# Block-sparse attention with a gated MLP: key and query loads ahead of values, a fourth raw buffer in the weight tile, one more probability buffer, split sums of squares

## Chip, core and metric

The kernel runs on one core of a Trainium2 chip. The metric is the device time of one execution in microseconds; lower is better. TensorE (PE) does matmuls and transposes, VectorE (DVE), ScalarE (ACT) and GpSimd (POOL) do the rest, and SyncE (SP) issues most of the DMAs. Each engine works through its own instructions in the order in which the program emits them.

## The reference

The inputs are q, k and v with batch 4, 8 heads, 768 positions and head size 64, a table of 3 sampled key blocks for each of 24 query blocks, and three weight matrices. All inputs but the table are 32-bit floats.

```python
scores = scale * np.matmul(q, k.transpose(0, 1, 3, 2))
# mask: window of one block, first and last block rows and columns, sampled blocks
scores = np.where(mask, scores, -1000000000.0)
attn = softmax(scores)
x = (attn @ v) as [B * S, H * D]           # 3072 x 512
xn = x / np.sqrt(np.mean(x * x, -1) + 1e-06) * rms_g
g = xn @ w_gate                            # 512 x 1536
out = (g * sigmoid(g) * (xn @ w_val)) @ w_out
```

## The kernel before, in words

Positions are laid out as 128 partitions by 6 columns. Heads are taken in pairs: each batch has 4 pairs, so g = 0 to 15 counts all pairs. The mask is not added to the scores: 24 extra rows of the contraction carry it, so keys and queries of a pair are cast into a tile `aug` of 88 used rows and then transposed into `X`. For batch 0 (pairs 0 to 3) PE transposes (`tpx`, L257) and a copy from PSUM follows (`evx`); the second half of the columns of the batch's queries comes by one load, `q2` (L227), and is cast and transposed later. For pairs 4 to 15 one DMA transpose a pair does it (`turn`, L243). Values are cast into `vaug` with a column of ones (`pad_v`).

The work is cut into 10 units: unit u has a batch and 1 or 3 query tiles of 128 (units 0 to 2 one each, unit 3 the other three tiles of batch 0, then two units of three tiles for each later batch). For every unit and pair there are score groups (`qk`, L275, two PSUM banks), exponentials on ACT (`exp`, L290), the product with the values (`av`, L304) and the division (`xo`, L315 and L316, DVE). Then come the sum of squares (`sq`, L326, DVE), its power -0.5 (`rsq`, L333, POOL), the scaled rows (`xq`, L340, DVE) and their transposition: for units 0 to 3 on PE with a copy (`tr`, L351, and `cp`, L359), for units 4 to 9 by a DMA transpose on SP's queue (`xt`, L366). The constant NPET is the first unit of the second kind. The MLP follows in groups f: `g` and `v` (L378), `th` (tanh, L387, ACT), `uu` (L393) and `hp` (L404, DVE), then `y` (L417) and the output (`yo`).

The order on each engine is made by a planner at build time. Every step is entered by `op` with the engines that may do it and a time for each, its dependences, a priority, and the buffers it takes and gives back; the planner picks the step that could start first, with priority breaking near ties. For DMAs a fixed list `seq` gives the order on SP's queue, in which DMA transposes stand where the planner puts them. What is planned is emitted in that order; the times in the plan are only for choosing.

Three buffers of the pool `raw` hold keys, queries and values as loaded. Pairs 0 to 2 of batch 0 have one each. Pair 3 takes the buffer of pair 0 (`load3`), so its load waits until pair 0's keys, queries and values have been cast. The weights are loaded by POOL in eight chunks of 384 columns (`wi`, L209) and two of `w_out` (L213). A small copy on POOL (`gate_pool`, L230) holds the first chunk until a load has landed; the third and fourth pair of chunks also wait for `rsq` of units 0 and 1. On SP a tiny DMA (`gate_sync`, L219) that reads a weight holds back the loads of pairs 4 to 7. The 40 unused columns of `aug` are cleared by POOL (`zero_pad`, L249) before pair 4 is cast.

Idle matmuls on a zero tile (L129) stand where the planner expects gaps on PE before 24 us.

Of the kernel before, what the change touches and what calls it, by code (L numbers as in the profile page):

```python
# [9 lines left out]
FP32 = mybir.dt.float32  # L10
BF16 = mybir.dt.bfloat16
# [6 lines left out]
def kernel(  # L18
# [12 lines left out]
    nc = tc.nc  # L31
# [14 lines left out]
    AHEAD, HURRY, HURU = 0.8, ("av", "xo", "sq", "rsq", "xq", "tr", "cp"), 0  # L46
    NSTARV = 3
    AH = {"uu": 0.3, "hp": 0.3}
# [51 lines left out]
    load0(1, 0)  # L100
    load0(0, 2)
    load0(1, 1)
# [126 lines left out]
    def gate_pool(g):  # L229
        nc.gpsimd.tensor_copy(out=scf, in_=A[g][:, 1, 0, 0:1])  # L230

# [14 lines left out]

    def zero_pad():
        for t in aug:
            nc.gpsimd.memset(t[:, :, :, :, KQ:P], 0.0)  # L249

# [29 lines left out]
    def exp(u, pr, g):  # L280
        b, c0, nt = UNITS[u]
        kt, w = KT[nt], nt * P
        if (u, pr) not in pts:
            if nt == 1:
                t_ = work.tile([P, 2, NC, 2, w], BF16, name="pt", tag="pt", bufs=NPT)
# [4 lines left out]
        nc.scalar.activation(  # L290
            out=pts[u, pr][:, g * kt:(g + 1) * kt].rearrange("p j e w -> p e j w"),
            in_=s_[:, :, 0:kt * w].rearrange("p e (j w) -> p e j w", w=w),
            func=AF.Exp, scale=SCALE)
# [26 lines left out]
    def sq(u, t):  # L320
        nt = UNITS[u][2]
        if u not in mss:
            mss[u] = work.tile([P, nt], FP32, name="ms", tag="ms")
        sc = work.tile([P, DM], BF16, name="sc", tag="sc", bufs=1)
        x = xos[u][:, t].rearrange("p h d -> p (h d)")
        nc.vector.tensor_tensor_reduce(  # L326
            out=sc, in0=x, in1=x, scale=1.0 / DM, scalar=1e-6, op0=ALU.mult, op1=ALU.add,
            accum_out=mss[u][:, t:t + 1])

    def rsq(u):  # L330
        nt = UNITS[u][2]
        r = work.tile([P, nt], FP32, name="rs", tag="rs")
        nc.gpsimd.tensor_tensor(out=r, in0=mss[u], in1=nhalf[:, 0:nt], op=ALU.pow)  # L333
        mss[u] = r
# [97 lines left out]

    NPT, NXN, NHP, NPET = 3, 3, 2, 4
    pools = {n: [0.0] * c for n, c in (
# [28 lines left out]

    def load3(e, p):
        A.append(raw.tile([P, 3, 2, NC * D], FP32, name="qkv", tag="qkv"))
        load0(3, 0)

# [3 lines left out]
    ld0(("l", 1, 0), 1.0)  # L471
    ld0(("l", 0, 2), 1.1)
    ld0(("l", 1, 1), 0.6)
    for g, i in ((2, 0), (2, 1), (1, 2), (3, 0), (3, 1), (2, 2), (3, 2)):
        ld0(("l", g, i), 0.6 if i == 1 else 1.1,
            load3 if (g, i) == (3, 0) else lambda e, p, g=g, i=i: load0(g, i),
            [], [("raw", 3)] if (g, i) == (3, 0) else [])
    ld0(("lg",), 0.7, lambda e, p: nc.sync.dma_start(
# [6 lines left out]
    for i in range(NWC + NOC):  # L485
        for m in range(2 if i < NWC else 1):
            def wi(e, p, i=i, m=m):
                if i + m == 0:
                    gate_pool(3)
                load_w(i, m) if i < NWC else load_wo(i - NWC)  # L490
            op(("wi", i, m), {"POOL": 0.9 + 0.2 * (i + m == 0)},
               [prev] if prev else [("l", 3, 0)], (2, i, m), wi)
            if (i, m) in ((2, 0), (3, 0)):
                made["wi", i, m]["deps"] += [("rsq", i - 2)]
            prev = ("wi", i, m)
        if i == 0:
            ld0(("q2",), 2.2, q2_, [], [("hp", ("q2",))])
            op(("w0",), {"DMA": 2.1}, [("wi", 0, 0)], (0,), None)
            seq.append(("w0",))
        op(("w", i), {"DMA": 4.2 if i else 2.1}, [prev], (0,), None)  # L500
        seq.append(("w", i))
        if i >= NWC - 1:
            seq += [("ld", NP + i - NWC + 1, j) for j in range(3)]
# [5 lines left out]
    for g in range(NP):  # L509
        a_ = g % NAUG  # L510
        rr = [("raw", g)]
        if g:
# [9 lines left out]
        for i in range(2):  # L522
            for n_, (es, lo, hi) in enumerate((KP, QP)[i][g == 0]):
                m_ = len(es) * (hi - lo)
                if i == 0:
                    pri = (-1, g, 0.5 + 0.1 * n_ + (g == 0 and lo == 3))
                else:
                    pri = (-1, g, 1) if lo == 0 else (2.5, g, lo)
                res = f"aK{a_}" if i == 0 else f"a{'QR'[lo == 3]}{a_}"
                key = ("tp", g, i, es[0], lo)  # L530
                op(key, {"PE": m_ * 0.056}, [("fq", g, lo)] if i else [("fk", g)] if g else [],
                   pri, lambda e, p, a=(g, i, es, lo, hi): tpx(*a, p),
                   [(TP1[:1] if i and lo == 3 else TP1, key), (f"X{g}", g)],
                   [(res, g)] if i == 0 else [(res, (g, lo == 3))])
# [14 lines left out]
    pools["aK0"] = []  # L549
    op(("zp",), {"POOL": 1.8}, [], (9,), lambda e, p: zero_pad(), at=24.0)  # L550
    for g in range(NP, B * NP):
        b, pr = divmod(g, NP)
        gate = {NP: 2, NP + 1: 3, NP + 2: 4, NP + 3: 5}.get(g)
        for i in range(3):
            def ld(e, p, g=g, i=i, gate=gate):
                if gate is not None and i == 0:
                    gate_sync(gate)
                load(g, i)
            op(("ld", g, i), {"DMA": 1.1}, [("w", gate)] if gate is not None and i == 0 else [],
               (1,), ld, [("raw", g)] if i == 0 else [])  # L560
            if i < 2:
                op(("fill", g, i), {"DVE": 0.57}, [("ld", g, i), ("zp",)] + [
                    ("tp", g_, i_, 0, 3 * i_) for g_ in (2, 3) for i_ in range(2)],
                   (4, g, i), lambda e, p, g=g, i=i: fill(g, i, e), [(f"aug{g % NAUG}", (g, False))])
# [16 lines left out]
    for u, (b, c0, nt) in enumerate(UNITS):  # L581
        w, last = nt * P, c0 + nt == NC
        ng = NC // KT[nt]
        for pr in range(NP):
            g0 = b * NP + pr
            pk = pr // 2 if nt == 1 else pr
            for g in range(ng):
                op(("qk", u, pr, g), {"PE": 2 * KT[nt] * mm(w)}, dep0(g0, b, c0, nt, KT[nt], g),
                   (2 if u else 0.5, u, pr, g), lambda e, p, a=(u, pr, g): qk(*a, p),
                   [(S3 if u < NOPEN else S_, ("s", u, pr, g)), ("pt", (u, pk))],  # L590
                   [(f"X{g0 % NSLOT}", g0)] if last and g == ng - 1 else [])
# [6 lines left out]
               lambda e, p, a=(u, pr): av(*a, p), [([(7,)] + [(6,)] * (u < 3), ("o", u, pr)), ("xo", u)],  # L598
               ([("pt", (u, pk))] if nt > 1 or pr % 2 else []) + ([(f"va{b % 2}", b)] if last and pr == NP - 1 else []))
            op(("xo", u, pr), {"DVE": 0.4 + w / 960.0}, [("av", u, pr)], (0, u, pr),  # L600
               lambda e, p, a=(u, pr): xo(*a), [], [(None, ("o", u, pr))])
        for t in range(nt):
            op(("sq", u, t), {"DVE": 0.75}, [("xo", u, pr) for pr in range(NP)], (1, u, t),
               lambda e, p, a=(u, t): sq(*a))
        op(("rsq", u), {"POOL": 0.9}, [("sq", u, t) for t in range(nt)], (0, u), lambda e, p, u=u: rsq(u))
        for t in range(nt):
# [82 lines left out]
    while ready:  # L689
# [27 lines left out]
        for names, key, nme in got:  # L717
# [11 lines left out]
        end[o["key"]] = fin + (  # L729
            3.7 if o["key"] == ("q2",) else 8.0 if o["key"][0] == "ld" and o["key"][1] >= NP else 4.0 if o["key"][0] == "turn"  # L730
            else LAT[e])
# [54 lines left out]
```

The softmax here doesn't subtract the row's maximum and nothing guards it: scores larger than these inputs give would overflow.

## Time and profile before

| what | value |
|---|---|
| median of 4 runs | 313.0 us (312.28 to 313.95) |
| profiled execution | 313.95 us |
| its span in the trace | 312.2 us |
| mean granted TensorE clock | 0.995 |
| PE waits for DVE, ACT in all | 3.8 us and 0.6 us |
| DMA queue of SP | 64800 packets, 37.23 MB |
| landing of a 384 KB load of keys, of values (median) | 4.6 us, 6.1 us |
| landing of a DMA transpose into `XA`, into `xn` (median) | 7.1 us, 3.7 us |

The span runs from the first to the last instruction of the trace. A group of instructions is given by line, engine, operation and tiles, with its count, busy time and mean. The sliced rows cut the span into 40 equal parts of 7.8 us; each digit is a busy share in tenths. PEclk is the granted clock of PE in tenths of full. The matmul ends are modelled, so busy time of PE is not a measure of how well it is used. In a timeline a line has start, duration, engine, line of code, operation and, in brackets, the idle time before it and what ended it.

### The profile page before, as it was taken

What the parts mean: (1) busy time and instruction counts of PE and PEld (TensorE: products, weight loads), DVE (VectorE), ACT (ScalarE), POOL (GpSimd) and SP (SyncE); (2) the same over time, 40 slices, a digit from 0 to 9 for tenths busy, and PEclk for the clock granted to TensorE, in tenths of its full rate; (3) what the DMA queues carried; (4) which work ended last, traced back from release to release, by engine and by line L of the source; (5) the groups of instructions that cost most, each with busy time, mean ns of one, the idle gap of its engine ahead of it and who ended that gap; (6) DMA issues with size and microseconds to landing.
All of it is one profiled execution on the core that took longest, in us unless ns stands there. A gap on an engine that the chain in (4) does not pass through costs nothing.

```text
span 312.2 us, 7395 instructions
## 1 busy us (share of the span) xinstructions
PE 303.9 (97%) x3063; PEld 201.8 (65%) x3063; DVE 191.1 (61%) x423; ACT 207.1 (66%) x325; POOL 24.6 (8%) x42
## 2 busy tenths in 40 slices
PE   8799999999999999999999999999999999999995
PEld 7798887866666666666666666666666546556543
DVE  5559655786666878766664853674488707727500
ACT  5958987678888777878787687878733233323222
POOL 3355500010000101000000100010001000000000
PEclk9979999999999999999999999999999999999999
DMA  6999999999999799951785030012000041010022
GB/s 206 304 236 166 168 267 236 164 300 294 252 258 240 255 208 251 285 177 36 151 140 100 34 84 4 34 21 66 2 34 3 6 121 60 0 68 2 0 104 101
DMA packets 70661, 42.42 MB, mean 136 GB/s; under 512 B 48356, under 2 KB 67556, under 8 KB 70628
## 3 DMA queue, kind: packets, MB, share of 16 engines
q1 hardware_dynamic: 64800, 37.23, 48.4%
q0 software_dynamic: 5792, 4.72, 10.0%
q8 instruction: 24, 0.39, 0.5%
q14 instruction: 9, 0.07, 0.1%
q10 hardware_dynamic: 36, 0.00, 0.0%
HBM read 28.57 MB, written 6.29 MB: 112 GB/s over the span
## 4 chain that ended last, share of the span: by engine, by line
PE 91%; DMA 3%; ACT 2%; DVE 1%; SPq 1%; issue 1%; ACTq 0%; DVEq 0%
PE PS L378 40%; PE PS L417 20%; PE PS L275 18%; PE PS L304 11%; DMA qkv<-in_k_dram 2%; DMA qkv<-in_v_dram 2%; ACT pt L290 2%; SPq L93 1%; PE PS L257 1%; PE PS L351 0%; ACT th L387 0%; DVE uu L393 0%; DVE aug L113 0%; ACT XA L109 0%; DVE vaug L113 0%
## 5 line engine op out<-in xcount | busy, mean ns | idle before, releaser
L290 ACT ACTIVATE pt<-PS 128x768 bf16<-128x768 f32 x192 | 145.6, 813 | 37.7 <-PE PS L275 36.2
L393 DVE SCALAR_TENSOR_TENSOR uu<-th,PS 128x384 bf16<-128x384 bf16 x96 | 53.2, 554 | 62.1 <-ACT th L387 59.9
L275 PE MATMUL PS<-XA 88*128 88x384 bf16 (+1 forms) x480 | 81.9, 296 | 0.7 <-ACT pt L290 0.6
L378 PE MATMUL PS<-xn,wg 128*128 128x384 bf16 (+1 forms) x480 | 75.4, 294 | 0.4 <-DVE uu L393 0.4
L378 PE MATMUL PS<-xn,wv 128*128 128x384 bf16 (+1 forms) x480 | 75.5, 293 | 0.0
L417 PE MATMUL PS<-wo,hp 128*128 128x512 bf16 (+1 forms) x300 | 70.4, 370 | 0.0
L387 ACT ACTIVATE th<-PS 128x384 bf16<-128x384 f32 x96 | 47.3, 493 | 33.0 <-PE PS L378 30.6
L404 DVE TENSOR_TENSOR hp<-uu,PS 128x384 bf16<-128x384 bf16 x96 | 51.4, 551 | 15.2 <-PE PS L378 14.4
L378 PEld LDWEIGHTS <-wg 128*128 128x128 bf16 x480 | 41.6, 97 | 24.1 <-issue 1.0
L378 PEld LDWEIGHTS <-wv 128*128 128x128 bf16 x480 | 41.5, 97 | 23.3 <-issue 0.2
L275 PEld LDWEIGHTS <-XA 88*128 88x128 bf16 x480 | 40.0, 99 | 21.6 <-issue 1.5
L417 PEld LDWEIGHTS <-hp 128*128 128x128 bf16 x300 | 29.0, 98 | 26.9
L304 PEld LDWEIGHTS <-pt 128*128 128x128 bf16 x1152 | 41.8, 98 | 6.0 <-issue 0.7
L304 PE MATMUL PS<-vaug,pt 128*128 128x65 bf16 x1152 | 43.3, 194 | 0.6 <-DVE xo L316 0.6
L427 ACT ACTIVATE yo<-PS 128x512 f32<-128x512 f32 (+1 forms) x23 | 13.3, 579 | 28.0 <-PE PS L417 27.1
L333 POOL TENSOR_TENSOR rs<-ms,nhalf 128x3 f32<-128x3 f32 (+1 forms) x10 | 7.8, 785 | 201.5 <-DVE ms L326 201.5
L316 DVE TENSOR_TENSOR xo<-PS,rz 128x384 f32<-128x384 f32 (+1 forms) x40 | 19.1, 478 | 1.4
L340 DVE SCALAR_TENSOR_TENSOR xq<-xo,rs,gB 128x512 bf16<-128x512 f32 x24 | 17.5, 754 | 0.2 <-POOL rs L333 0.2
L315 DVE RECIPROCAL rz<-PS 128x6 f32<-128x6 f32 (+1 forms) x40 | 7.4, 185 | 16.1 <-PE PS L304 16.0
L113 DVE CAST aug<-qkv 128x768 bf16<-128x768 f32 (+2 forms) x30 | 15.2, 524 | 3.1 <-DMA qkv<-in_k_dram 2.7
L326 DVE CUSTOM_DVE_ANT_0 sc<-xo 128x512 bf16<-128x512 f32 x24 | 16.5, 687 | 0.3
L257 PE MATMUL PS<-ident,aug 128*88 128x128 bf16 x96 | 8.4, 239 | 1.9 <-DVE XA L113 1.7
(54 smaller groups left out, 70.1 us busy)
## 6 DMA issues: line engine op xcount, KB each, us to landing
qkv<-in_v_dram SPq DMA_DIRECT2D x16, 384.0 KB, 6.1
out_dram<-yo SPq DMA_DIRECT2D x23, 256.0 KB, 2.0
qkv<-in_k_dram SPq DMA_DIRECT2D x15, 384.0 KB, 4.6
qkv<-in_q_dram SPq DMA_DIRECT2D x12, 384.0 KB, 4.7
wg<-in_moe_w_gate_dram POOLq DMA_DIRECT2D x4, 384.0 KB, 6.6
wv<-in_moe_w_val_dram POOLq DMA_DIRECT2D x4, 384.0 KB, 8.1
wo<-in_moe_w_out_dram POOLq DMA_DIRECT2D x2, 768.0 KB, 17.4
q<-in_q_dram SPq DMA_DIRECT2D x1, 768.0 KB
```

The costliest lines, as they stand in the source:

```text
L113: nc.vector.tensor_copy(out=out, in_=in_)
L275: nc.tensor.matmul(out=s_[:, e, j * w:(j + 1) * w], lhsT=x[0:KQ, 0, e, jt * P:(jt + 1) * P], rhs=x[0:KQ, 1, e, c0 * P:c0 * P + w], start=T ...
L290: nc.scalar.activation(out=pts[u, pr][:, g * kt:(g + 1) * kt].rearrange("p j e w -> p e j w"), in_=s_[:, :, 0:kt * w].rearrange("p e (j w) ...
L304: nc.tensor.matmul(out=o_[:, t, e, :], lhsT=pt[:, jt, e, t * P:(t + 1) * P], rhs=va[:, (2 * pr + e) * NC + jt, 0:D + 1], start=(jt == 0), ...
L316: nc.vector.tensor_tensor(out=xos[u][:, :, 2 * pr:2 * pr + 2, :], in0=o_[:, :, :, 0:D], in1=rz.unsqueeze(3).to_broadcast([P, nt, 2, D]), o ...
L326: nc.vector.tensor_tensor_reduce(out=sc, in0=x, in1=x, scale=1.0 / DM, scalar=1e-6, op0=ALU.mult, op1=ALU.add, accum_out=mss[u][:, t:t + 1])
L340: nc.vector.scalar_tensor_tensor(out=xqs[u][:, t, :], in0=xos[u][:, t].rearrange("p h d -> p (h d)"), scalar=mss[u][:, t:t + 1], in1=gB, o ...
L378: nc.tensor.matmul(out=p_[:, j, :].rearrange("p (t w) -> p t w", w=P), lhsT=w_[:, c, f_ * P:(f_ + 1) * P], rhs=xns[u][:, :, c, :], start=( ...
L387: nc.scalar.activation(out=t_, in_=tiles["gp", u, f], func=AF.Tanh, scale=0.5)
L393: nc.vector.scalar_tensor_tensor(out=t_, in0=tiles.pop(("th", u, f)), scalar=1.0, in1=tiles.pop(("gp", u, f)), op0=ALU.add, op1=ALU.mult)
L404: nc.vector.tensor_tensor(out=hps[u][:, f * fg:(f + 1) * fg, :], in0=tiles.pop(("uu", u, f)), in1=tiles.pop(("vp", u, f)), op=ALU.mult)
L417: nc.tensor.matmul(out=tiles["yp", u, t, h], lhsT=hps[u][:, f, t * P:(t + 1) * P], rhs=wo[:, f, x], start=(f == 0), stop=(f == NF - 1))
```

## The change

Loads of batch 0 are issued in the order k0, q0, k1, q1, k2, q2, k3, q3, then v0 to v3; before, v0 stood ahead of q1, and v1 ahead of k3. Pair 3's raw data lie in the first 4608 columns of the tile `wo`, seen as 32-bit floats, which the load of `w_out` fills later; `load3` and its wait for a buffer are gone. The first weight chunk waits for the values of pair 1 instead of the queries of pair 3.

The probabilities of pairs 2 and 3 of unit 0 are put into a buffer of the pool `hp` (`ph`), so units 0 to 2 have four such buffers and not three. For units 0 to 2 the sum of squares is taken in two instructions, the first over the first three pairs, the second over the last pair with the first result as its start. The columns of `aug` are cleared by DVE, one tile at a time, not before 32 us of the plan. The copies of the second half of the queries of pairs 0 to 3 can be done by DVE only, and their transposes may use a second PSUM bank. Gate groups of unit 3 may use a second bank. NPET is 2, so the transposes of units 2 and 3 go by DMA on SP's queue. The plan reckons with 2.6 us from issue to landing for the later loads of batch 0.

In the program that results PE has 16 transposes (L351) and 2 idle matmuls fewer. All casts of the second half of the queries are on POOL. In SP's queue unit 2's DMA transpose stands directly behind the load `q2` and ahead of the gate and loads of pair 4. Behind it come the loads of pairs 4 and 5, `turn` of pairs 4 and 5, an output, and then the gate and three loads of pair 6, the gate and the keys of pair 7, unit 3's DMA transpose, an output, two loads of pair 7, three of pair 8 and `turn` of pair 6. On PE the first matmuls with values come behind 13 of the score groups, where it was 5. The order of the first gate group of unit 3 and the score groups of pairs 5 and 6 has also moved.

```diff
-    load0(0, 2)
     load0(1, 1)
...
-        nc.gpsimd.tensor_copy(out=scf, in_=A[g][:, 1, 0, 0:1])
+        nc.gpsimd.tensor_copy(out=scf, in_=A[g][:, 2, 0, 0:1])
...
-    def zero_pad():
-        for t in aug:
-            nc.gpsimd.memset(t[:, :, :, :, KQ:P], 0.0)
+    def zero_pad(i):
+        nc.vector.memset(aug[i][:, :, :, :, KQ:P], 0.0)
...
+                if u == 0 and pr == 2:
+                    t_ = work.tile([P, NF, 3 * P], BF16, name="ph", tag="hp", bufs=NHP)
...
+        i, z = 0 if nt == 1 else t, slice(0, DM)
+        if nt == 1:
+            z = (slice(0, 3 * DM // 4), slice(3 * DM // 4, DM))[t]
+        x = xos[u][:, i].rearrange("p h d -> p (h d)")[:, z]
         nc.vector.tensor_tensor_reduce(
-            out=sc, in0=x, in1=x, scale=1.0 / DM, scalar=1e-6, op0=ALU.mult, op1=ALU.add,
-            accum_out=mss[u][:, t:t + 1])
+            out=sc[:, z], in0=x, in1=x, scale=1.0 / DM, scalar=mss[u][:, 0:1] if nt == 1 and t else 1e-6,
+            op0=ALU.mult, op1=ALU.add, accum_out=mss[u][:, t:t + 1])
...
-    NPT, NXN, NHP, NPET = 3, 3, 2, 4
+    NPT, NXN, NHP, NPET = 3, 3, 2, 2
...
-    def load3(e, p):
-        A.append(raw.tile([P, 3, 2, NC * D], FP32, name="qkv", tag="qkv"))
-        load0(3, 0)
+    A.append(wo.rearrange("p f x -> p (f x)")[:, 0:12 * NC * D].bitcast(FP32).rearrange(
+        "p (i e x) -> p i e x", i=3, e=2))
...
-    for g, i in ((2, 0), (2, 1), (1, 2), (3, 0), (3, 1), (2, 2), (3, 2)):
+    for g, i in ((2, 0), (2, 1), (3, 0), (3, 1), (0, 2), (1, 2), (2, 2), (3, 2)):
...
-               [prev] if prev else [("l", 3, 0)], (2, i, m), wi)
+               [prev] if prev else [("l", 1, 2)], (2, i, m), wi)
...
-                   [(TP1[:1] if i and lo == 3 else TP1, key), (f"X{g}", g)],
+                   [(TP1[:2] if i and lo == 3 else TP1, key), (f"X{g}", g)],
...
-                elif i and lo == 3 or g == 0 and lo == 0:
+                elif g == 0 and lo == 0:
...
-    op(("zp",), {"POOL": 1.8}, [], (9,), lambda e, p: zero_pad(), at=24.0)
+    for i in range(2):
+        op(("zp", i), {"DVE": 0.4}, [], (9,), lambda e, p, i=i: zero_pad(i), at=ZPAT)
...
-               lambda e, p, a=(u, f): proj(*a, wg, "gp", p), [([(4,)], ("g", u, f)), ("hp", HG[u])])
+               lambda e, p, a=(u, f): proj(*a, wg, "gp", p), [([(4,)] + [(6,)] * (2 < u < NG2), ("g", u, f)), ("hp", HG[u])])
```

More of the change, by code (lines that the diff above doesn't have):

```diff
@@ L46 @@
     AHEAD, HURRY, HURU = 0.8, ("av", "xo", "sq", "rsq", "xq", "tr", "cp"), 0
-    NSTARV = 3
+    NSTARV, ZPAT, NG2 = 3, 32.0, 4
     AH = {"uu": 0.3, "hp": 0.3}
@@ L284, in exp @@
             if nt == 1:
-                t_ = work.tile([P, 2, NC, 2, w], BF16, name="pt", tag="pt", bufs=NPT)
+                if u == 0 and pr == 2:
+                    t_ = work.tile([P, NF, 3 * P], BF16, name="ph", tag="hp", bufs=NHP)
+                    t_ = t_.rearrange("p f w -> p (f w)")[:, 0:4 * NC * w].rearrange(
+                        "p (a j e w) -> p a j e w", a=2, j=NC, e=2)
+                else:
+                    t_ = work.tile([P, 2, NC, 2, w], BF16, name="pt", tag="pt", bufs=NPT)
                 pts[u, pr // 2 * 2], pts[u, pr // 2 * 2 + 1] = t_[:, 0], t_[:, 1]
@@ L322, in sq @@
         if u not in mss:
-            mss[u] = work.tile([P, nt], FP32, name="ms", tag="ms")
+            mss[u] = work.tile([P, max(nt, 2)], FP32, name="ms", tag="ms")
         sc = work.tile([P, DM], BF16, name="sc", tag="sc", bufs=1)
-        x = xos[u][:, t].rearrange("p h d -> p (h d)")
+        i, z = 0 if nt == 1 else t, slice(0, DM)
+        if nt == 1:
+            z = (slice(0, 3 * DM // 4), slice(3 * DM // 4, DM))[t]
+        x = xos[u][:, i].rearrange("p h d -> p (h d)")[:, z]
         nc.vector.tensor_tensor_reduce(
-            out=sc, in0=x, in1=x, scale=1.0 / DM, scalar=1e-6, op0=ALU.mult, op1=ALU.add,
-            accum_out=mss[u][:, t:t + 1])
+            out=sc[:, z], in0=x, in1=x, scale=1.0 / DM, scalar=mss[u][:, 0:1] if nt == 1 and t else 1e-6,
+            op0=ALU.mult, op1=ALU.add, accum_out=mss[u][:, t:t + 1])
     def rsq(u):
@@ L332, in rsq @@
         r = work.tile([P, nt], FP32, name="rs", tag="rs")
-        nc.gpsimd.tensor_tensor(out=r, in0=mss[u], in1=nhalf[:, 0:nt], op=ALU.pow)
+        x = mss[u][:, 1:2] if nt == 1 else mss[u]
+        nc.gpsimd.tensor_tensor(out=r, in0=x, in1=nhalf[:, 0:nt], op=ALU.pow)
         mss[u] = r
@@ L471 @@
     ld0(("l", 1, 0), 1.0)
-    ld0(("l", 0, 2), 1.1)
     ld0(("l", 1, 1), 0.6)
-    for g, i in ((2, 0), (2, 1), (1, 2), (3, 0), (3, 1), (2, 2), (3, 2)):
+    for g, i in ((2, 0), (2, 1), (3, 0), (3, 1), (0, 2), (1, 2), (2, 2), (3, 2)):
         ld0(("l", g, i), 0.6 if i == 1 else 1.1,
-            load3 if (g, i) == (3, 0) else lambda e, p, g=g, i=i: load0(g, i),
-            [], [("raw", 3)] if (g, i) == (3, 0) else [])
+            lambda e, p, g=g, i=i: load0(g, i))
     ld0(("lg",), 0.7, lambda e, p: nc.sync.dma_start(
@@ L488, in wi @@
                 if i + m == 0:
-                    gate_pool(3)
+                    gate_pool(1)
                 load_w(i, m) if i < NWC else load_wo(i - NWC)
             op(("wi", i, m), {"POOL": 0.9 + 0.2 * (i + m == 0)},
-               [prev] if prev else [("l", 3, 0)], (2, i, m), wi)
+               [prev] if prev else [("l", 1, 2)], (2, i, m), wi)
             if (i, m) in ((2, 0), (3, 0)):
@@ L510 @@
         a_ = g % NAUG
-        rr = [("raw", g)]
+        rr = [("raw", g)] if g < NP - 1 else []
         if g:
@@ L561 @@
             if i < 2:
-                op(("fill", g, i), {"DVE": 0.57}, [("ld", g, i), ("zp",)] + [
+                op(("fill", g, i), {"DVE": 0.57}, [("ld", g, i), ("zp", 0), ("zp", 1)] + [
                     ("tp", g_, i_, 0, 3 * i_) for g_ in (2, 3) for i_ in range(2)],
@@ L586 @@
             pk = pr // 2 if nt == 1 else pr
+            ptn = ("hp", "ph") if u == 0 and pk == 1 else ("pt", (u, pk))
             for g in range(ng):
@@ L589 @@
                    (2 if u else 0.5, u, pr, g), lambda e, p, a=(u, pr, g): qk(*a, p),
-                   [(S3 if u < NOPEN else S_, ("s", u, pr, g)), ("pt", (u, pk))],
+                   [(S3 if u < NOPEN else S_, ("s", u, pr, g)), ptn],
                    [(f"X{g0 % NSLOT}", g0)] if last and g == ng - 1 else [])
@@ L598 @@
                lambda e, p, a=(u, pr): av(*a, p), [([(7,)] + [(6,)] * (u < 3), ("o", u, pr)), ("xo", u)],
-               ([("pt", (u, pk))] if nt > 1 or pr % 2 else []) + ([(f"va{b % 2}", b)] if last and pr == NP - 1 else []))
+               ([ptn] if nt > 1 or pr % 2 else []) + ([(f"va{b % 2}", b)] if last and pr == NP - 1 else []))
             op(("xo", u, pr), {"DVE": 0.4 + w / 960.0}, [("av", u, pr)], (0, u, pr),
                lambda e, p, a=(u, pr): xo(*a), [], [(None, ("o", u, pr))])
-        for t in range(nt):
-            op(("sq", u, t), {"DVE": 0.75}, [("xo", u, pr) for pr in range(NP)], (1, u, t),
+        ns = max(nt, 2)
+        for t in range(ns):
+            dq = [("sq", u, 0)] if nt == 1 and t else []
+            d_ = 0.75 if nt > 1 else (0.6, 0.25)[t]
+            op(("sq", u, t), {"DVE": d_}, dq + [("xo", u, pr) for pr in range(NP - (nt == 1 and t == 0))], (1, u, t),
                lambda e, p, a=(u, t): sq(*a))
-        op(("rsq", u), {"POOL": 0.9}, [("sq", u, t) for t in range(nt)], (0, u), lambda e, p, u=u: rsq(u))
+        op(("rsq", u), {"POOL": 0.9}, [("sq", u, t) for t in range(ns)], (0, u), lambda e, p, u=u: rsq(u))
         for t in range(nt):
@@ L729 @@
         end[o["key"]] = fin + (
-            3.7 if o["key"] == ("q2",) else 8.0 if o["key"][0] == "ld" and o["key"][1] >= NP else 4.0 if o["key"][0] == "turn"
+            3.7 if o["key"] == ("q2",) else 2.6 if o["key"][0] == "l" and (o["key"][1] > 1 or o["key"][2] == 2) else 8.0 if o["key"][0] == "ld" and o["key"][1] >= NP else 4.0 if o["key"][0] == "turn"
             else LAT[e])
```

## The prediction

> **What bounds the kernel now.** I read the busy rows and the sliced rows of the page first, then the waits of TensorE, then the first 40 us in the timeline and in windows of 1 us, then the landing times of the DMAs.
>
> ```profile
> PE 303.9 (97%) x3063; PEld 201.8 (65%) x3063; DVE 191.1 (61%) x423; ACT 207.1 (66%) x325; POOL 24.6 (8%) x42
> ...
> PE   8799999999999999999999999999999999999995
> ...
> PEclk9979999999999999999999999999999999999999
> DMA  6999999999999799951785030012000041010022
> ```
>
> TensorE is busy nearly everywhere; only the first slices and the third digit of the granted clock stand out. But busy is not useful. From the chain of waits I take back-to-back rates: 12 matmuls of 128 columns in 0.67 us, 4 of 384 in 0.65, 36 of 65 in 1.15, 3 of 512 in 0.65. By these the 84 transposes, 144 small score matmuls, 132 value matmuls, 12 gate matmuls and 4 `xq` transposes ahead of the first score of unit 3 (the 384-wide L275 at 30.66 us) are 4.7+8.0+4.2+0.7+0.2 = 17.8 us of work, while 30.66-4.72 = 25.9 us pass from the first transpose. So 8.1 us of PE time are lost before 30.7 us. From there to 308.5 us it hardly waits. A gain must come from those 8.1 us, or from taking work off PE.
>
> Where they are lost (timeline, PE alone, then windows of the early stretch: busy us by engine, PEclk, DMA share, GB/s):
>
> ```profile
> 13.73 0.49 PE L275 MATMUL PS<-XA 88*128 88x128 bf16 x6 [0.21 <-ACT pt L290]
> 15.97 1.27 PE L257 MATMUL PS<-ident,aug 128*88 128x128 bf16 x16 [1.75 <-DVE XA L113]
> ```
>
> ```profile
> 14.00:15.00 1.00, 0.23 (x5) 0.05 (x1) 0.41 (x1) 1.00 (x3) 0.00 (x0) 1.00 1.17 242
> 15.00:16.00 1.00, 0.03 (x1) 0.14 (x2) 1.00 (x4) 0.79 (x2) 0.94 (x2) 1.00 0.83 197
> ...
> 17.00:18.00 1.00, 1.00 (x13) 1.00 (x12) 1.00 (x3) 0.00 (x0) 1.00 (x3) 0.50 0.99 304
> 18.00:19.00 1.00, 1.00 (x21) 1.00 (x20) 0.35 (x3) 0.81 (x1) 1.00 (x2) 0.50 1.21 284
> ```
>
> PE stands still, then runs at half clock until about 20.3 us, and ACT (fourth number) starves at 16 to 18. The source is one load: keys of pair 3 use the buffer of pair 0, so SP issues them only after pair 0's values are padded:
>
> ```profile
> 9.04 0.37 SPq L93 DMA_DIRECT2D qkv<-in_k_dram  x1
> ```
> ```profile
> 14.59 0.87 DVE L113 CAST aug<-qkv 128x768 bf16<-128x768 f32 x2 [2.07 <-DMA qkv<-in_k_dram]
> ```
>
> Issued 9.04, landed 14.55. The second loss is a DVE cast beside a GpSimd memset:
>
> ```profile
> 26.85 2.57 DVE L113 CAST aug<-q 128x384 bf16<-128x384 f32 x1
> ```
> ```profile
> 27.44 1.76 POOL L249 MEMSET aug<- 128x960 bf16 x2
> ```
>
> A cast of this form takes 0.35 us elsewhere. It ends with the memset, and PE waits 0.58 us for the DVE step behind it (L304, at 29.88).
>
> **The change, part by part.** *Loads (gain).* Pair 3's keys and queries no longer wait for a buffer: they lie in the weight tile, free until its own load, and all key and query loads go ahead of the values. In the trace k0 and q0 (576 KB) are in at 6.0 us, and eight loads (2,496 KB) at about 11.6: 343 KB per us. At that rate k3 (2,112 KB in all) lands at 10.5, q3 at 11.0, v0 at 12.2, v1 13.3, v2 14.4. k3 gains 4 us. v0 comes 4 us later than its 8.3, but the changed program puts the first value matmuls behind 13 score groups, of which three can be ahead of ACT, so ten exponentials come before (0.74 us each from 7.41: 14.8 us). So the delay is hidden; if the score groups were slower to come it would cost up to 4 us, but then ACT has work.
>
> With no gap ACT sets the pace. In before, 24 exponentials of units 0 to 2 run from 7.41 to 30.30; their rows take 4.48+3.62+0.81+6.48+1.53+0.85 = 17.8 us. The rest is 3.8 us idle and three other operations. After: 17.8, one 0.59 copy, one 0.5 tanh, and 0.5 for small gaps put the end near 26.8, and the first score of unit 3 at 26.5 instead of 30.66. The same PE operations precede it in both programs, idle matmuls aside, so the gain is **4.2 us**. Bounds: 2 (new waits on DVE copies) to 4.9 (no gaps).
>
> *Clock.* TensorE: Matmul & The Clock Gate ("Part 1: The HAM clock gate") says the clock halves after an idle window of about 3.4 us. Here 2.6 us with 0.5 us of work in them (13.4 to 16.0) came before 3.7 us of half clock. By either, PE work of 80% of the time (some 13.5 us of it in 8.5 to 25.5 after) should keep full clock. This is inside the 4.2, not on top.
>
> *Memset moved to DVE, queries' second halves left to POOL, copies left to DVE.* The memset's stall goes (inside the 4.2). DVE takes two memsets (a DVE memset of 144 columns takes 0.178 and one of 48 0.098, so about 0.86 for 960; POOL needed 0.92), three copies of 0.55 that ACT did at 0.79, and gives up one cast of 0.35: 3.0 us more. From 19 to 33 us of before DVE was idle 3.6 of 14 us and stalled 2.2. At zero, since PE does not wait for the memsets until pair 4; without that cover, up to 2 us (this is rival (b)). SBUF - State Buffer ("SBUF: two separate sides") speaks against leaving casts on POOL: DVE in a two-port mode and GpSimd lock each other out for a whole instruction. The 2.57 us row agrees; but POOL's casts are 0.50 us, so a block costs at most 0.5 a time against 2.2 there.
>
> *Fourth probability buffer.* Pair 2 and 3 of unit 0 use an `hp` buffer, held early only by the second query half: removes a possible wait, adds none before the first gate matmul. Zero. The second PSUM bank for these transposes and for unit 3's gate groups likewise only adds a choice. *Split squares.* Three units each get a second instruction and accumulator read: 0.69+0.08 becomes some 0.55+0.08+0.25+0.08, with the first part before the last pair. Three times 0.2 us more DVE, 0.4 shorter chain; zero.
>
> *Weights.* Their first issue waits for v1 (13.3) and not q3 (15.06); the third and fourth chunk wait for `rsq` 0 and 1, which come some 4 us sooner. In before the DMA moved only 86 to 90 GB/s at 27 to 29 and 33 to 35, so there is room. The load of `wo` now also waits for pair 3's casts, which are done by about 18 us, while POOL reached it at 32.97 in before; behind it on POOL stands only unit 2's `rsq`. Zero; if a chunk is late, up to 1 us.
>
> *Transposes of units 2 and 3 leave PE (gain).* 16 PE transposes: 4 at 0.056 and 12 in 0.70: **0.9 us**. ACT loses copies of 0.62 and 1.44.
>
> *The DMA transposes that take their place (loss).* They go on SP's queue. Unit 2's stands ahead of the gate and three loads of pair 4; it waits for `xq` 2, about 32 us, and these loads went at 34.06 in before, so they stay put; its consumer comes some 18 us later. Zero, up to 1 us should pair 4 come late. Unit 3's is tight. Ahead of its first gate matmuls the changed program puts, after the last `v` of unit 2's third group, 4 `y` groups, 7 score groups, a `g`, a `v` and one `av`: 2.6+2.3+0.7+0.7+1.15 = 7.4 us. Of these DVE needs 0.65 for the product ahead and 2.1 for three `xq`. 4.5 us are left. And:
>
> ```profile
> xn<-xq SPq DMA_TRANSPOSE x6, 3.7
> ```
>
> 3.7 in the quiet part, 5.2 for the one behind six loads issued up to 3.8 us before (at 124.85). In the changed order it is issued directly behind the three loads of pair 6 and one of pair 7; loads in such a burst landed 6.8 after issue (65 to 67 us in before), up to 8.6. DMA: Bandwidth & Descriptors ("Queues, rings and completion order") has descriptors consumed in ring order, so four loads ahead are 1,536/343 = 4.5 us before it starts. By the lone row it costs 0, by 5.2 0.7, by the burst 2.3. I take 6.0, between the two: **1.5 us lost**. Bounds 0 and 4.1.
>
> Sum: 4.2+0.9-1.5 = 3.6 us. The profiled execution was 313.95 us, span 312.2 and 1.75 around it: 310.35. The median of the four runs lies 0.95 below it: **309.4 us**.
>
> **Rivals.** (a) *Nothing lost at unit 3* and the small stalls near 104 to 111 us also shrink by 0.5: 313-4.2-0.9-0.5 = 307.4. For: landings of 3.7 are usual; against: the burst. 0.22. (b) *Start gains half*: DVE's copies or a weight chunk become the next bound: 313-2-0.9+1.5 = 311.6. For: DVE is in order, and has waits for v1 and v2 in the middle of its copies; against: its idle time. 0.18. (c) *SP's queue turns the sign*: unit 3's transpose waits behind the burst, lands 9 to 10 us after `xq` (a transpose in before took 9.0) and costs 5; the transpose of pair 6 queues behind it, and its scores had under 2 us to spare in before, so 2 more: 313-5.1+7 = 314.9. It decides once the two stalls pass 5.1 us. For: the same queue, 4.9 to 7 us per big transpose at SP; against: pair 6's scores are planned 2.5 us of work later. 0.12. The forecast (308 to 310.8) has 0.48.
>
> **Numbers.** A measurement of this kernel tells about 0.5% (1.6 us) from no change. Faster: 0.48+0.22 and a third of (b): 0.76. Same: the rest of (b), some of (c): 0.14. Slower: 0.10. Range 306.7 to 313.0: (a), the forecast and (b).
>
> **What would show it.** Right: no PE wait near 14 to 16, PEclk whole in the third slice, unit 3's first score near 26.5, a PE gap ahead of the first 384-wide `wg` matmul with a DMA as its releaser, 16 fewer PE transposes. Wrong: exponentials still pausing before 26 us (load step), a half clock early, a landing of `xn` under 4.5 us (then 1.5 us less) or over 7, PE waits on DVE at 18 to 26.

## The result and the profile after

| | before | after |
|---|---|---|
| median | 312.11 us (53 runs, 310.84 to 315.76) | 309.95 us (32 runs, 309.02 to 317.71) |
| profiled execution, its span | 313.95, 312.2 us | 310.08, 308.4 us |
| first 384-wide score of unit 3 | 30.66 us | 25.59 us |
| last `y` group begins | 293.44 us | 289.70 us |

The ratio is 0.9928, with a 95% interval of 0.9913 to 0.9943: 2.2 us faster. A few executions of either kernel run at a lower granted clock and take longer; the ratios leave them out, and one trace of such an execution (314.78 us) is read below only for one wait and the clock behind it.

The two profiled executions differ by 3.87 us, more than the medians. That gap is a part of the story.

The page of the kernel after, its busy rows, the PE and clock rows of the slices, and the DMA row:

```profile
PE 300.5 (97%) x3045; PEld 198.7 (64%) x3045; DVE 190.8 (62%) x432; ACT 203.2 (66%) x320; POOL 24.6 (8%) x42
...
PE   8999999999999899999999999999999999999995
...
PEclk9999999999999999999999999999999999999999
DMA  7999999999999999940694060103000040020022
```

The dent in the third clock digit is gone. PE has 18 matmuls fewer. A new dent stands in PE's fourteenth digit, 100 to 108 us. The waits of PE name it; columns are total us, times, longest us:

```profile
PE PS L385 <- DMA xn<-xq: 2.0, 2, 1.8
PE PS L128 <- DVE zt L115: 1.1, 1, 1.1
PE PS L273 <- ACT pt L293: 0.8, 3, 0.3
PE PS L385 <- DVE uu L400: 0.2, 1, 0.2
```

The waits of before for DVE (1.7 for `XA`, 0.6 for `xo`) are gone. In their place PE waits 2.0 us for DMA transposes: 0.15 at unit 3, 1.82 at unit 4. In the timeline of PE:

```profile
14.32 0.49 PE L273 MATMUL PS<-XA 88*128 88x128 bf16 x6
14.66 0.55 PE L307 MATMUL PS<-vaug,pt 128*128 128x65 bf16 x12
15.10 0.51 PE L273 MATMUL PS<-XA 88*128 88x128 bf16 x6
...
25.59 0.49 PE L273 MATMUL PS<-XA 88*128 88x384 bf16 x2
...
66.46 0.82 PE L385 MATMUL PS<-xn,wg 128*128 128x384 bf16 x4 [0.15 <-DMA xn<-xq]
...
108.36 0.81 PE L385 MATMUL PS<-xn,wg 128*128 128x384 bf16 x4 [1.82 <-DMA xn<-xq]
```

Between 14 and 16 us, where before stood still, PE now has no idle time in brackets at all. SP's queue ahead of the second of these waits:

```profile
97.25 0.57 SPq L80 DMA_DIRECT2D qkv<-in_q_dram  x1
97.87 0.47 SPq L80 DMA_DIRECT2D qkv<-in_v_dram  x1
98.45 0.40 SPq L80 DMA_DIRECT2D qkv<-in_k_dram  x1
99.31 0.37 SPq L80 DMA_DIRECT2D qkv<-in_q_dram  x1
99.75 0.45 SPq L80 DMA_DIRECT2D qkv<-in_v_dram  x1
102.35 2.32 SPq L373 DMA_TRANSPOSE xn<-xq  x1
```

Five loads stand ahead of unit 4's DMA transpose. It was issued at 102.35, and PE's matmuls on it began at 108.36: 6.0 us later, where before's were 3.7 apart (107.73 to 111.43).

A ledger of the profiled pair, from PE's timelines, after minus before. First score of unit 3: -5.07. Sixteen PE transposes: -0.89. Losses from there to 66 us: +0.94 net. From 66 us to unit 4's first gate matmul: 2.22 lost after and 0.91 before, +1.31. Later stages are alike. The sum is -3.71; the last `y` moved by -3.74. The first score of unit 3 is a fair mark for this pair: the same 84 transposes, 144 score, 132 value, 12 gate and 4 `xq` matmuls stand ahead of it in both programs.

### The profile page after: what moved, and what is told of

Its sections match the earlier page's. It is cut to its first block, busy times and chain, and to the rows that moved or that the text cites. A ratio compares the mean times of both kernels' runs of the same rounds, so it can differ in the third digit from the quotient of the medians.

```text
span 308.4 us, 7343 instructions
## 1 busy us (share of the span) xinstructions
PE 300.5 (97%) x3045; PEld 198.7 (64%) x3045; DVE 190.8 (62%) x432; ACT 203.2 (66%) x320; POOL 24.6 (8%) x42
## 4 chain that ended last, share of the span: by engine, by line
PE 90%; DMA 5%; DVE 1%; ACT 1%; SPq 1%; issue 0%; ACTq 0%; DVEq 0%
PE PS L385 40%; PE PS L424 19%; PE PS L273 18%; PE PS L307 11%; DMA xn<-xq 4%; DMA qkv<-in_k_dram 2%; PE PS L255 1%; SPq L93 1%; ACT pt L293 1%; DVE xq L347 1%; ACT yo L434 0%; PE PS L128 0%; DVE aug L112 0%; DVE uu L400 0%; DVE xo L319 0%
## 5 line engine op out<-in xcount | busy, mean ns | idle before, releaser
L293 ACT ACTIVATE pt<-PS 128x768 bf16<-128x768 f32 x188 | 142.9, 811 | 32.4 <-PE PS L273 31.9
L273 PE MATMUL PS<-XA 88*128 88x384 bf16 (+1 forms) x480 | 81.0, 293 | 0.8 <-ACT pt L293 0.8
L411 DVE TENSOR_TENSOR hp<-uu,PS 128x384 bf16<-128x384 bf16 x96 | 51.4, 551 | 14.8 <-PE PS L385 14.5
L307 PEld LDWEIGHTS <-pt 128*128 128x128 bf16 x1128 | 40.2, 97 | 5.4
L307 PE MATMUL PS<-vaug,pt 128*128 128x65 bf16 x1128 | 41.7, 193 | 0.0
L332 DVE CUSTOM_DVE_ANT_0 sc<-xo 128x512 bf16<-128x512 f32 (+1 forms) x24 | 16.1, 670 | 0.3
L112 DVE COPY XA<-PS 88x768 bf16<-88x768 bf16 (+2 forms) x16 | 8.2, 529 | 2.2 <-PE PS L255 1.9
```

The costliest lines, as they stand in the source:

```text
L112: nc.vector.tensor_copy(out=out, in_=in_)
L273: nc.tensor.matmul(out=s_[:, e, j * w:(j + 1) * w], lhsT=x[0:KQ, 0, e, jt * P:(jt + 1) * P], rhs=x[0:KQ, 1, e, c0 * P:c0 * P + w], start=T ...
L293: nc.scalar.activation(out=pts[u, pr][:, g * kt:(g + 1) * kt].rearrange("p j e w -> p e j w"), in_=s_[:, :, 0:kt * w].rearrange("p e (j w) ...
L307: nc.tensor.matmul(out=o_[:, t, e, :], lhsT=pt[:, jt, e, t * P:(t + 1) * P], rhs=va[:, (2 * pr + e) * NC + jt, 0:D + 1], start=(jt == 0), ...
L332: nc.vector.tensor_tensor_reduce(out=sc[:, z], in0=x, in1=x, scale=1.0 / DM, scalar=mss[u][:, 0:1] if nt == 1 and t else 1e-6, op0=ALU.mul ...
L411: nc.vector.tensor_tensor(out=hps[u][:, f * fg:(f + 1) * fg, :], in0=tiles.pop(("uu", u, f)), in1=tiles.pop(("vp", u, f)), op=ALU.mult)
```

## The experiments

Four accounts were held against each other. **A**: the load step alone makes the start's gain, and the wait at unit 4 comes from the order as planned. **B**: the DVE step (memset, late copies, second bank) makes half of it or more, and the two steps add. **C**: the new DMA transposes of units 2 and 3 push SP's queue and so cause the wait at unit 4. **D**: the profiled executions of before are longer than usual, so part of the profiled gain is not in the medians.

**The load step alone, on the kernel before** (with the weights' gate on pair 1's values and 2.6 us for these loads in the plan).

```diff
-    load0(0, 2)
...
-        nc.gpsimd.tensor_copy(out=scf, in_=A[g][:, 1, 0, 0:1])
+        nc.gpsimd.tensor_copy(out=scf, in_=A[g][:, 2, 0, 0:1])
...
+    A.append(wo.rearrange("p f x -> p (f x)")[:, 0:12 * NC * D].bitcast(FP32).rearrange(
+        "p (i e x) -> p i e x", i=3, e=2))
...
-    for g, i in ((2, 0), (2, 1), (1, 2), (3, 0), (3, 1), (2, 2), (3, 2)):
+    for g, i in ((2, 0), (2, 1), (3, 0), (3, 1), (0, 2), (1, 2), (2, 2), (3, 2)):
...
-        rr = [("raw", g)]
+        rr = [("raw", g)] if g < NP - 1 else []
```

> The kernel before with the load step alone: pair 3's raw data in the weight tile, keys and queries ahead of values, first weight chunk behind the values of pair 1. Theory A (the load step carries the start): PE's stop near 14 to 16 us and the half clock are gone, the memset's 0.6 us wait stays, ACT still makes the late copies; the first score of unit 3 near 27.5 us (30.66 before), a ratio of 0.990 to 0.993. Theory B (the DVE and POOL side carries the start): the first score comes no earlier than 29.5 us and the ratio is 0.996 or more.

Measured: 310.3 us, ratio 0.9922 [0.9891, 0.9953]. Its first score of unit 3 stands at 26.49, and its last `y` at 289.45. In its PE timeline around 14 us there is neither a stop nor half clock. A is borne out in so far as this one step, by itself, gives as much as the whole change does (0.9928). The rest of the change does nothing on top of it in the medians, which the experiments below take apart.

The mark has to be read with care here, since the planner has moved work across it: 12 gate matmuls more and 6 transposes fewer stand ahead of it than in before, 0.3 us of work in all at the rates of the prediction. With before's work ahead of it, it would stand near 26.2 (an estimate).

**The DVE step alone, on the kernel before.**

```diff
-        for t in aug:
-            nc.gpsimd.memset(t[:, :, :, :, KQ:P], 0.0)
+        nc.vector.memset(aug[i][:, :, :, :, KQ:P], 0.0)
...
-                   [(TP1[:1] if i and lo == 3 else TP1, key), (f"X{g}", g)],
+                   [(TP1[:2] if i and lo == 3 else TP1, key), (f"X{g}", g)],
...
-                elif i and lo == 3 or g == 0 and lo == 0:
+                elif g == 0 and lo == 0:
```

> The kernel before with the clearing of aug on DVE and the late copies of queries on DVE alone, with the second PSUM bank for their transposes, but the old loads. Theory A: the stop near 14 to 16 us stays, the 2.57 us cast is gone; 0.5 to 1 us gained, a ratio of 0.997 to 0.999. Theory B: 2 to 3 us gained, a ratio of 0.991 to 0.994.

Measured: 310.61 us, 0.9942 [0.9907, 0.9977]; first score of unit 3 at 26.15. A's number for it (0.997 to 0.999) missed, and B's (0.991 to 0.994) was nearly met. The matmuls of PE come in before's order until about 22 us of this trace (25 us of before's), and yet its stop was short:

```profile
14.77 1.17 PE L256 MATMUL PS<-ident,aug 128*88 128x128 bf16 x18 [0.58 <-DVE XA L113]
```

Before's stop there was 1.75. The earlier start is thus partly that execution's own. It is also partly a change of order: 24 value and 12 gate matmuls that stand ahead of the first score of unit 3 in before stand behind it here, and 6 transposes have come ahead of it, 1.1 us of work less; with before's work it would stand near 27.25 (an estimate). What the edit itself plainly takes away is the stall behind the memset (the wait for `xo`, 0.6 in before, is gone).

**Both steps, without the rest.** The two edits above together.

> The kernel before with the load step and the DVE step together, but without the fourth probability buffer, the split squares, the second bank for unit 3's gates and the DMA transposes of units 2 and 3. If the two gains at the start add up, the first score of unit 3 comes at 24.5 us or earlier and the time is 308 or less. If both remove the same wait (ACT then sets the pace), the first score comes near 25.6 to 26.3 as in the changed kernel, and the time is 309.5 to 310.5.

Measured: 310.27 us, 0.9941 [0.9914, 0.9968]; first score at 25.14, and a wait of 1.09 for `xn` at unit 4. The medians do not add, against B: the ratios are 0.9922, 0.9942 and, for both, 0.9941. The starts nearly do. Ahead of the first score of unit 3 this kernel has 12 gate matmuls fewer and 6 transposes more than before, so with before's work it would stand near 25.5. The four estimates, from a start of before with a short stop (28.23, in the trace of the longer landing on the kernel before, below): load step 2.1 us earlier, DVE step 1.0 (0.2 of it its shorter stop), both 2.8, the kernel after 2.6. What both gained at the start did not reach the end; the wait at unit 4, which neither step's own trace shows and this one does, is 1.09 us of it. That it explains the rest of the difference is not shown.

**Units 2 and 3 back on PE, on the kernel after.**

```diff
-    NPT, NXN, NHP, NPET = 3, 3, 2, 2
+    NPT, NXN, NHP, NPET = 3, 3, 2, 4
```

> The changed kernel with units 2 and 3 transposed on PE again (NPET 4). Theory A (the DMA transposes give 0.9 us of PE work and cost waits of about 2 us in all, of which unit 4's is there anyway): 0 to 1 us slower than the changed kernel, near 310.5; unit 4 still waits for its DMA transpose, 1 to 2 us. Theory C (the two new DMA transposes crowd SP's queue and so cause unit 4's wait): unit 4 does not wait, and the time is 0.5 to 1 us shorter than the changed kernel's, near 309.

Measured: 312.28 us, 0.9981 [0.9949, 1.0013]. The wait at unit 4 is there without any of the new DMA transposes:

```profile
109.41 0.81 PE L385 MATMUL PS<-xn,wg 128*128 128x384 bf16 x4 [1.75 <-DMA xn<-xq]
```

C falls. But A had asked for 310.5 with this edit, 0.9 us of PE work; the medians of after and of this kernel are 2.3 apart (1.7 by the ratios), while in the traces the last `y` is 1.04 later (290.74 to 289.70). Five of this kernel's 12 executions had a granted clock of 0.995 or less, and the median of the other seven is 311.43; the rest was not found.

**Unit 4 on PE as well** (NPET = 5).

> The changed kernel with units 2, 3 and 4 transposed on PE (NPET 5). This adds 28 PE transposes (12+12+4 at 0.056 to 0.06 us, 1.6 us) to the changed kernel and takes away every wait for an xn landing that its trace shows (2.0 us). Theory A: about 0.4 us shorter than the changed kernel, near 309.5; no wait for xn near 106 us. Theory C as in the run with NPET 4, but then no better than that run (0.7 us of PE work more).

Measured: 310.19 us, 0.9918 [0.9886, 0.995], where A said 309.5; PE waits for no DMA any more. Against the kernel after, PE has 28 transposes more (3073 matmuls against 3045): 4 and 24 at the rates of the prediction are 1.6 us of work. Waits of 2.0 us went. The medians are 0.2 us apart. So as planned here the three DMA transposes saved what their waits took.

**The kernel before and the kernel after, once more.** No edit.

> The kernel before once more, unchanged, for a second trace. Theory D (the profiled execution of before was a poor one: the values of pair 0 landed late, the keys of pair 3 after them, PE stood still long enough for the half clock): here the keys of pair 3 are issued earlier than 9.04 us, the stop near 14 to 16 us is under 1 us, no half clock after it, and the span is near 310.5 us with the first score of unit 3 near 28.5. Rival: the stop and the half clock come each time, and the first score stays near 30.7 us.

> The changed kernel once more. If the wait of 1.8 us at the first gate matmul of unit 4 belongs to its order and not to one execution, it is there again (1.3 us or more), and at unit 3 there is at most 0.5 us. Ratio 0.991 to 0.994, span near 308.4. If it was chance, the wait is under 0.7 us and the span near 307.

Before came out at 315.13 us, with its stop (1.72 us) and half clock again, so D was not borne out here. PE also waited 1.06 us for `xn` at unit 4, which the first trace of before does not show:

```profile
112.56 0.81 PE L378 MATMUL PS<-xn,wg 128*128 128x384 bf16 x4 [1.06 <-DMA xn<-xq]
```

After had a median of 309.96 us, 0.9932 [0.9902, 0.9963]. Its trace is of a long execution; its longest wait is at the same place, and this time the clock went to half behind it:

```profile
110.09 1.44 PE L385 MATMUL PS<-xn,wg 128*128 128x384 bf16 x4 [3.55 <-DMA xn<-xq]
```

```profile
110.00:111.00 1.00, 0.91 (x3) 0.41 (x3) 0.00 (x0) 0.00 (x0) 0.00 (x0) 0.50 1.24 292
```

**A longer landing in the plan, on the kernel after.** The plan gives a DMA transpose into `xn` 1.8 us on the queue and 1.9 behind it, 3.7 from issue; this edit makes it 6.3. Nothing else is touched, and nothing is put off by hand: only the order that the planner picks can change.

```diff
-            3.7 if o["key"] == ("q2",) else 2.6 if o["key"][0] == "l" and (o["key"][1] > 1 or o["key"][2] == 2) else 8.0 if o["key"][0] == "ld" and o["key"][1] >= NP else 4.0 if o["key"][0] == "turn"
+            3.7 if o["key"] == ("q2",) else 4.5 if o["key"][0] == "cp" and e == "DMA" else 2.6 if o["key"][0] == "l" and (o["key"][1] > 1 or o["key"][2] == 2) else 8.0 if o["key"][0] == "ld" and o["key"][1] >= NP else 4.0 if o["key"][0] == "turn"
```

> The changed kernel with one number of the plan changed: a DMA transpose into xn is reckoned to land 4.5 us after its issue and not 1.9, so that the plan puts more PE work ahead of the first gate group: between the last value product of unit 4 and its first gate group 16.3 us of PE work instead of 12.7 (unit 3: 15.9 instead of 12.6). If the wait for xn is a true loss, 2.0 us go: near 308, a ratio near 0.986, no wait for xn in the trace. If other waits take its place (exponentials or products that now come late), 309.5 to 310.

Measured: 308.26 us (307.81 to 308.76), 0.9862 [0.9833, 0.9891]: the fastest version of all, 1.7 us under the kernel after, as expected. No wait for `xn`, although unit 4's transpose landed 6.1 us after its issue at 102.02. PE had other work in the meantime:

```profile
106.70 0.81 PE L424 MATMUL PS<-wo,hp 128*128 128x512 bf16 x3
107.35 0.49 PE L273 MATMUL PS<-XA 88*128 88x384 bf16 x2
107.68 0.81 PE L424 MATMUL PS<-wo,hp 128*128 128x512 bf16 x3
108.33 0.49 PE L273 MATMUL PS<-XA 88*128 88x384 bf16 x2
108.65 0.81 PE L424 MATMUL PS<-wo,hp 128*128 128x512 bf16 x3
109.30 0.49 PE L273 MATMUL PS<-XA 88*128 88x384 bf16 x2
109.63 0.65 PE L385 MATMUL PS<-xn,wg 128*128 128x384 bf16 x3
```

**The same with units 2 and 3 on PE** (NPET = 4 and the longer landing).

> The changed kernel with units 2 and 3 transposed on PE (NPET 4) and with the plan's landing of 4.5 us, so that unit 4 has 17.4 us of PE work between its last value product and its first gate group. Beside the run with that landing and NPET 2 (308.3) this is the value of the two DMA transposes with the wait at unit 4 gone from both. Theory A (they give the 16 PE transposes, 0.9 us): 309.2. If they give nothing once covered: 308.3. If they did harm: under 308.

Measured: 310.49 us, 0.993 [0.9898, 0.9961]; no wait for `xn`. So with the wait out of the way, the DMA transposes of units 2 and 3 are worth 0.9930-0.9862 = 0.0068, 2.1 us. The PE work is 0.9 of it; in this trace the first score of unit 3 stands at 26.68 against 25.97, 0.7; the rest is open.

**The kernel after without the fourth probability buffer, the split squares and unit 3's second bank** (the load and DVE steps, NPET = 2 and the longer landing, on the kernel before).

> The kernel before with the load step, the DVE step, NPET 2 and the plan's landing of 4.5 us: all of the change but the fourth probability buffer, the split squares and the second bank for unit 3's gates, beside the run that has them (308.3). As predicted (they are worth nothing): 308.3 within 0.5. If they carry part of the gain: 309 or more.

Measured: 312.36 us, 0.9975 [0.994, 1.0011]. Its profiled execution is its fastest, 310.18 us, and has no wait for `xn`. Against the fastest version its last `y` is 1.35 us later in the trace (289.45 to 288.10), and 0.0113, 3.5 us, in the medians. These edits, which the prediction put at zero, seem to be worth something here, in the planner's hands at least; why the timed runs of this kernel lie 2 us above its trace stays open. Nor can such worths be added up: this kernel is the one with both steps (0.9941) plus NPET = 2 and the longer landing, and it was no faster for them.

**The longer landing alone, on the kernel before.**

> The kernel before with the plan's landing of 4.5 us alone. The start is as in before. If before loses time at unit 4 too in most executions (about 0.9 us between 66 and 111 us in its trace), a ratio of 0.996 to 0.998; if only the changed order is exposed, 1.0 within 0.002.

Measured: 312.9 us, 1.0012 [0.9983, 1.0041]; no wait for `xn`, but no gain either, as expected if only the changed order were exposed. The time from the first score of unit 3 to the end did not get shorter, and where it was lost instead was not looked for. So the longer landing is no cure by itself. The traced execution (312.91 us) lies on the median, and its start, which is before's program, shows a short stop:

```profile
15.02 1.16 PE L257 MATMUL PS<-ident,aug 128*88 128x128 bf16 x18 [0.80 <-DVE XA L113]
```

Its first score of unit 3 stands at 28.23, not 30.66.

**The kernel before, a third time.** No edit.

> The kernel before once more, unchanged, timed, for a trace of an execution near its median of 312.1. Theory D in its weaker form (two traces of before so far, 313.95 and 315.13, both with the stop of 1.7 us near 14 us and the half clock; its median is 312.1): an execution at 312.1 has a stop under 1 us and no half clock, with a span near 310.4. Rival: the stop and the half clock are there at 312.1 too, and what is missing from the median lies later (the wait at unit 4).

Measured: 311.74 us, and 0.9959 [0.9931, 0.9988] against other runs of the very same kernel. So one batch's interval understates what is left: differences of about 0.4% say little. Its traced execution was again a long one, 314.12 us, with the stop and, at unit 4, the wait:

```profile
16.08 1.11 PE L257 MATMUL PS<-ident,aug 128*88 128x128 bf16 x17 [1.81 <-DVE XA L113]
...
111.58 0.81 PE L378 MATMUL PS<-xn,wg 128*128 128x384 bf16 x4 [1.27 <-DMA xn<-xq]
```

A trace of before at 312.1 us was not caught.

## Why the prediction was right, and where it was off

The number, 309.4 us, lies 0.55 below the median of 309.95, but that closeness is partly luck. It took 3.6 us from 313.0; the medians of all runs differ by 2.2 from a base of 312.1. The signs of the terms were right, and two sizes were not: the start was put at 4.2 where 2.6 is nearer (below), and the loss at unit 3 at 1.5 where 0.3 came. A loss at unit 4, which no term had, stood in for the second.

**Load step: right, in mechanism and times.** The estimated landings against POOL's and DMA's own rows: k3 10.5, and the cast that waited for it began at 10.82; v0 12.2 (12.32), v1 13.3 (13.35). The first value matmuls began at 14.66 (at 14.8 or later by the estimate). ACT's exponentials waited for scores 0.8 us in the first 26 us, where they had waited 4.4 in the first 30. "4.2 us" was 5.07 in the profiled pair. Half a microsecond of that is an earlier first exponential (6.89 against 7.41), whose two loads are the first in both programs. The clock stayed whole, as argued; the half clock of before lasted 3.41 us in its trace, where the prediction read 3.7.

**The size of the base: off.** Before's stop is no constant. Up to the stop the same order of work ran in five traces, with stops of 1.75, 1.72, 1.81, 0.80 and 0.58 us and first scores of unit 3 at 30.66, 30.36, 29.30, 28.23 and 26.15 (the last with another order behind 22 us and without the memset stall). The first three are the kernel before itself, in executions of 313.95, 315.13 and 314.12 us, all above its median; the fourth lies on its own. With 28.23 the start gains 28.23-25.59 = 2.6 us, not 5.1. The granted clocks on record say how common the half clock is. The profiled execution of before had a mean of 0.995. Of 87 repeated executions of before, 69 had 0.997 or more, with a median of 312.1 us, and 15 had 0.994 or 0.995, with a median of 314.4. So the stretch at half clock that the prediction saw is not in most executions of before, and the mean clock accounts for some 1.5 us of the profiled gain (0.005 of 312.2, an estimate), which is most of the step from 3.87 to 2.2. That short stops are the rule in before's median executions too is argued from these traces, not shown, as no execution of before at its median was traced; before's third trace had a long stop at whole clock. Nor does the first idea of D, that a second look would show the shorter stop, stand.

**PE transposes: right** (0.9; 0.89).

**The DMA transpose of unit 3: the wrong landing.** Its cover of 4.5 us was right (4.73 passed between issue and wait); it landed after 4.8, not 6.0, and cost 0.15 of wait and 0.17 of gap. The failed step is the use of the ring order: "four loads ahead are 1,536/343 = 4.5 us before it starts". The four loads were issued 4.3 to 2.2 us ahead of the transpose (57.25 to 59.43 against 61.58), and by the prediction's own rate, counted from the first of these issues, they were done at 57.25+4.5 = 61.7. Counted so, hardly any delay was left for the transpose.

**Unit 4: missed.** The prediction looked for a new wait at the transposes that the change adds. It came at one that both programs have. The wait is the landing less the work that the plan puts in between:

| kernel | issue | work in between | landing | wait |
|---|---|---|---|---|
| before, first trace | 107.73 | 3.70 | up to 3.70 | 0 |
| before, second trace | 107.83 | 3.67 | 4.73 | 1.06 |
| before, third trace | 106.64 | 3.67 | 4.94 | 1.27 |
| both steps | 102.17 | 4.43 | 5.52 | 1.09 |
| after, NPET 4 | 104.61 | 3.05 | 4.80 | 1.75 |
| after | 102.35 | 4.19 | 6.01 | 1.82 |
| after, 6.3 us in the plan | 102.02 | 7.61 | 6.1 | 0 |

(Work in between is the first gate matmul's start less its idle time and the issue; landing is that start less the issue, where PE waited.) The planner fills about the 3.7 us that it was told, and the transposes land 3.7 to 6.1 us after issue. So the wait was in before too, in two traces of three, and the trace that the prediction had was the one without it. In the kernel after, all of it goes when the plan is told the longer time, and the median falls by 1.7 us. What makes a landing 6.0 and not 3.7 is not settled: five loads ahead, by the rate of 343 KB per us, would end at 97.25+1920/343 = 102.85, half a microsecond after the issue.

**Put at zero.** The memset on DVE: it took 0.97 us for both tiles (0.86 estimated), at 32.14, and no PE wait is near: right. Buffers, second bank and split squares: wrong, by the run without them.

**Rivals.** (a), nothing lost at unit 3, was nearly so, but the loss stood at unit 4. (b), that DVE or a weight chunk holds the start to 2 us, is not seen as a wait; yet its size was nearer than the forecast's: it gave 1.4 us in all and the forecast 3.6, and 2.2 came. (c), SP's queue turning the sign, did not decide; its mechanism, a long landing of `xn`, is what the 3.55 us show.

## What to carry to other kernels

An order made by a planner depends on the latencies it is told. Compare them with the landings of a DMA transpose under load, not with the quiet one alone, before judging a change that uses more of them; but measure the result, since the same longer figure gave 1.7 us on one kernel and nothing on the other. Two cures for one stage can add up at that stage and still not at the end, where a later wait takes the gain. A mark in a timeline compares two programs only where the same work stands ahead of it. Take the stall that a change is to remove from several executions, and look at their granted clocks; one profiled execution may hold a longer stall than the median does.

## What was not expected of the hardware

- The clock halved behind stops of 1.75 and 1.72 us, but not behind one of 1.81 at the same place. The last is plain in the windows of before's third trace; the number ahead of the DMA share is the granted clock:

```profile
16.00:17.00 1.00, 0.92 (x17) 0.92 (x17) 0.97 (x5) 0.00 (x0) 1.00 (x2) 1.00 1.02 342
17.00:18.00 1.00, 1.00 (x30) 1.00 (x27) 1.00 (x3) 0.38 (x1) 1.00 (x3) 1.00 1.06 292
```

  The length of a stop alone did not decide here. Where the stop lay seems to: in the traces the stretches of one clock last 3.41 us or a multiple of it (10.24, then 3.41 at half clock, in before's first two traces; 102.4, then 6.83, in the long execution of after). On that grid, counted from the first rise of the clock, the stretches that came before a half clock held PE work for 43, 53 and 18% of their time; before's third stop fell across two stretches, with 73 and 68%. No simple limit comes out of it, as the stretch with the wait at unit 4 in the kernel with NPET = 4 held 49% and was followed by whole clock. As for a rule: the idle window of about 3.4 us that the Trainium skill gives (TensorE: Matmul & The Clock Gate, "Part 1: The HAM clock gate") was not reached by any of the three stops.
- While PE waited for unit 4's transpose, the DMA engines were almost idle for a microsecond, at a share of 0.07 and 7 GB/s, in the windows of the kernel after:

```profile
105.00:106.00 1.00, 1.00 (x6) 0.48 (x5) 0.97 (x3) 0.81 (x2) 0.00 (x0) 1.00 2.45 118
106.00:107.00 1.00, 0.54 (x3) 0.19 (x2) 0.59 (x2) 1.00 (x3) 0.00 (x0) 1.00 0.07 7
107.00:108.00 1.00, 0.00 (x0) 0.00 (x0) 0.00 (x0) 0.41 (x1) 0.00 (x0) 1.00 1.09 287
```

  So in that microsecond it was not loads that held the transpose up; no run here took it further.
